# A hi/lo-split attention and gated MLP kernel: a new order for its whole program, from the first loads on, and eleven operations that change engine

## The chip, the cores and the metric

One core of a Trainium2 chip runs the kernel. The metric is the device time in microseconds (us) of one execution. The kernel before takes 412.66 us, the median of three runs (412.56 to 412.87).

## The reference

All arithmetic is float32; S = 2048 tokens, D = 512, F = 1376, 32 heads of 16.

```python
xn = layernorm(x)
q, k, v = split_heads(xn @ wqkv)                # 32 heads, Dh = 16
idx = pos[:, None] - arange(8) * 2              # window 8, dilation 2, causal
logits = einsum("bhsd,bhswd->bhsw", q, k[idx]) * Dh ** -0.5
s = einsum("bhsw,bhswd->bhsd", softmax(logits), v[idx]) @ wo
g = silu(gelu(layernorm(xn) @ w1 + b1) @ w2 + b2)
out = x + s * g
```

## The kernel before

**Split operands.** The large matmuls run in f16. Each operand is kept as a high half, the value rounded to f16, and a low half, what is left. A product is the sum of three matmuls: high by high, low by high, high by low. So each tile of an operand costs a pass for its high half (on ScalarE, or by table on VectorE or GpSimd) and one for its low half (mostly on VectorE).

**Tiles and stages.** The 2048 tokens are taken as two dilation halves of 8 tiles of 128 tokens. The 512 columns of q, k and v are taken as 4 head blocks; head block and half make 8 attention units. Of each unit TensorE makes q, k and v of the 8 tiles (`qkv`, matmul L864: 12 per tile, 384 columns, 480 where one head block also carries a piece of the MLP's last columns), and the PSUM result is evicted with its scale into the array `U`, on VectorE (L878) or ScalarE (L882, and L886 for the extra 96 columns). For units 0 and 1 the tables `EV0` and `EV1` name the engine per tile; from unit 2 on it is ScalarE. Logits, softmax (Exp at L956) and weighted sums run on VectorE and GpSimd. The MLP runs beside this in 4 chunks of 512 tokens: `mlp1` makes a block of h (L1143, 12 matmuls of 512 columns), ScalarE applies Gelu in PSUM (L1156) and writes the high half (L1159), `mlp2` multiplies by w2 (L1186). L1056 and L1088 are the output product with wo. The PSUM tiles of L864, L1143 and L1056 come from one ring of three buffers, ps0 to ps2.

**The opening.** Loads are issued by SyncE in one queue: `t` (L1258, 256 KB) is a tile of x that comes transposed, for tiles 6 and 7; `x` (L1233, 256 KB) is a tile of x in rows; `q` (L588, 384 KB) is a quarter of wqkv for head block 0; `w` (L1260) are pieces of w1. Tiles 6 and 7 take the direct way: their mean is made on VectorE (L685) and one matmul (L691), or for tile 7 with four matmuls (L682); L693 subtracts it, and L700 multiplies float32 x by float32 wqkv, one matmul per tile and quarter (two records each in the trace). The other tiles get statistics on VectorE (L659, L660), a power on GpSimd (L718), a normalisation (L748 on GpSimd, L742 and L744 on ScalarE, or L751 on VectorE), and a transpose on TensorE (L766, four per tile), whose result is split into halves in `yT` (L770 ScalarE or L772 VectorE for the high half, by `HI_ENG`; L773 for the low). The square sums of wqkv's quarters are made on ScalarE (L597) and summed on TensorE (L513); VectorE makes a power of two of them (L524 to L542), by which the high halves of wqkv are scaled (L619). Before the data come, TensorE runs 19 matmuls of no use (L1305). w1's high halves are made by `split` on ScalarE (L565) or VectorE (L563), by the table `W1ENG`.

**What sets the order.** Each operation is entered into a plan with its engine, reads and writes. `Plan.issue` then emits all of them in the sequence that the long table `ORDER` gives, one number per operation. Each engine's program is that sequence, cut down to its own instructions, and the buffers of a ring are handed out in it as well, so ORDER also decides which PSUM buffer a product gets. At run time each engine works through its list in order and waits by semaphores.

```python
HI_ENG = ('act', 'act', 'act', 'dve', 'dve', 'dve', 'dve', 'act')      # L53
W1ENG = ('act', 'dve', 'act', 'act', 'act', 'act', 'act')              # L57
EV0 = ('act', 'dve', 'dve', 'act', 'act', 'act', 'dve', 'dve')         # L62
EV1 = ('dve', 'dve', 'act', 'act', 'act', 'act', 'dve', 'act')         # L63
order, fixed = [], [self.ops[n] for n in reversed(ORDER)]              # Plan.issue
```

## Time and profile before

| | |
|---|---|
| timed runs, median (lowest to highest) | 412.66 us (412.56 to 412.87) |
| profiled execution: span, first to last instruction | 411.0 us |
| TensorE (PE) busy, matmuls | 402.8 us, 98%, 2030 records |
| VectorE (DVE) busy | 381.6 us, 93% |
| ScalarE (ACT) busy | 224.9 us, 55% |
| GpSimd (POOL) busy | 132.7 us, 32% |

The page gives a span for the profiled execution and no time beyond it; the median of the runs is 1.66 us longer than that span. Busy shares are means over the whole span: ScalarE, at 55% overall, is full in some stretches and idle in others. In a timeline row the figure in brackets is how long the engine stood idle before the row, and what ended that. The start times of successive rows on TensorE show its pace better than the durations, since a matmul's record reaches into the next one's.

### The profile page before, as it was taken

Reading aid. Unit: us, or ns where it says so; the run is one execution under the profiler, and the core shown is the slowest. Engines: PE = TensorE matmul, PEld = TensorE weight load, DVE = VectorE, ACT = ScalarE, POOL = GpSimd, SP = SyncE. Lnnn points to the kernel's source line nnn. Section 1 sums busy time; section 2 is a strip of 40 time slices with the busy share of each in tenths; the row PEclk is TensorE's granted clock in tenths of the full one; section 3 lists DMA queues with packets and bytes.
Section 4 is the critical chain, followed back from the end, with each engine's and each line's share of the span. In section 5 each row is a group of like instructions: output and inputs, shape, how many; then the busy total and the mean of one; then the engine's idle time right before and its main releaser. Section 6 shows DMA issues by size and latency. Waiting matters only on the chain.

```text
span 411.0 us, 5490 instructions
## 1 busy us (share of the span) xinstructions
PE 402.8 (98%) x2030; PEld 198.7 (48%) x2030; DVE 381.6 (93%) x386; ACT 224.9 (55%) x372; POOL 132.7 (32%) x141
## 2 busy tenths in 40 slices
PE   7899999999999999999999999999999999999996
PEld 4565544444444455445544554444445544444443
DVE  4899999999999999999889999899999989989985
ACT  3899987983989736633564164214523177236310
POOL 2843000053562425143424243233322505250012
PEclk9999999999999999999999999999999999999999
DMA  8957538251018372911251009610344452004984
GB/s 288 395 104 227 177 90 214 92 179 27 1 30 189 85 130 77 150 49 27 51 141 27 0 2 213 209 50 22 107 122 120 107 135 60 0 1 116 285 214 162
DMA packets 52627, 48.04 MB, mean 117 GB/s; under 512 B 37066, under 2 KB 37510, under 8 KB 52088
## 3 DMA queue, kind: packets, MB, share of 16 engines
...
q8 instruction: 16, 0.26, 0.3%
...
## 4 chain that ended last, share of the span: by engine, by line
PE 90%; DVE 3%; ACT 3%; DMA 1%; POOL 1%; issue 0%; SPq 0%; POOLq 0%; ACTq 0%; DVEq 0%
PE ps L864 27%; PE z L1186 25%; PE ps L1143 25%; PE ps L1056 5%; PE z L1088 2%; PE ps L1088 2%; PE z L1174 2%; DMA prod<-in_A_x_dram 1%; DVE bn L659 1%; ACT w L565 1%; ACT w L504 1%; PE pl L1088 1%; PE z L1177 1%; PE pl L864 1%; POOL prod L748 1%; DVE yT L773 0%
## 5 line engine op out<-in xcount | busy, mean ns | idle before, releaser
L864 PE MATMUL ps<-wq,yT 128*128 128x384 f16 (+1 forms) x708 | 128.9, 337 | 0.2
L1186 PE MATMUL z<-w,h 128*128 128x512 f16 x480 | 111.4, 379 | 0.0
L1143 PE MATMUL ps<-yT,w 128*128 128x512 f16 x480 | 109.0, 379 | 0.0
L864 PEld LDWEIGHTS <-yT 128*128 128x128 f16 x744 | 72.2, 98 | 59.1 <-issue 1.3
L930 DVE TENSOR_TENSOR prod<-U 128x2048 f32<-128x2048 f32 x32 | 73.8, 2312 | 4.1 <-ACT U L882 3.0
L1143 PEld LDWEIGHTS <-w 128*128 128x128 f16 x480 | 46.8, 98 | 55.6 <-issue 0.5
L933 DVE TENSOR_REDUCE L<-prod 128x128 f32<-128x2048 f32 x32 | 73.0, 2282 | 0.5
L1186 PEld LDWEIGHTS <-h 128*128 128x128 f16 x480 | 46.5, 98 | 54.6 <-issue 0.7
L999 POOL TENSOR_TENSOR prod<-prod,prod 128x1024 f32<-128x1024 f32 x14 | 41.3, 2968 | 81.3 <-DVE prod L988 81.3
L882 ACT ACTIVATE U<-ps,cs 128x384 f32<-128x384 f32 x54 | 30.1, 575 | 62.9 <-PE ps L864 62.7
L988 DVE TENSOR_TENSOR prod<-pl,U 128x2048 f32<-128x2048 f32 x28 | 63.5, 2283 | 0.3
L1156 ACT ACTIVATE ps<-ps,b1T,hsc 128x512 f32<-128x512 f32 x40 | 29.8, 747 | 37.0 <-PE ps L1143 36.8
L1159 ACT ACTIVATE h<-ps,hsc 128x512 f16<-128x512 f32 x40 | 27.4, 684 | 20.6 <-PE z L1186 19.7
L1009 POOL COPY gate<-prod 1x1 f32<-1x1 f32 x21 | 4.6, 219 | 102.2 <-DVE prod L930 102.2
L1010 POOL TENSOR_TENSOR prod<-prod 128x1024 f32<-128x1024 f32 x14 | 32.9, 2348 | 0.0
L1161 DVE SCALAR_TENSOR_TENSOR h<-ps,hsc,h 128x512 f16<-128x512 f32 x40 | 29.5, 744 | 3.2 <-ACT h L1159 3.2
L1056 PE MATMUL ps<-wo,oT 128*128 128x512 f16 x96 | 21.5, 379 | 0.0
L983 DVE TENSOR_TENSOR prod<-prod,prod 128x2048 f32<-128x2048 f32 x9 | 20.6, 2288 | 0.2
L971 ACT ACTIVATE o<-prod,osc 128x1024 f16<-128x1024 f32 (+1 forms) x9 | 9.5, 1051 | 18.0 <-DVE prod L983 9.9
L1010 POOL TENSOR_TENSOR prod<-prod,prod 128x1024 f32<-128x1024 f32 x7 | 16.4, 2347 | 0.0
L1088 PEld LDWEIGHTS <-oT 128*128 128x128 f16 x108 | 10.5, 98 | 10.4 <-issue 0.2
L1056 PEld LDWEIGHTS <-oT 128*128 128x128 f16 x96 | 9.4, 98 | 11.1
...
## 6 DMA issues: line engine op xcount, KB each, us to landing
...
```

The source lines that it names most:

```text
L864: nc.tensor.matmul(b.t[:, 0:wide], y[:, s, k, o:o + P], wq[hb][:, t, k], start=(n == 0), stop=(n == 11))
L882: act(384, lambda i=i, b=b: nc.scalar.activation(U3[:, i:i + 31:15, :], b.t[:, 0:384].rearrange("p (t e) -> p t e", t=3), AF.Identity, sca ...
L930: dve(2048, lambda p2=p2, g=g: nc.vector.tensor_tensor(p2(), q, slots(Ut, KH, 2 * g), op=ALU.mult), qk + [("kh", ub, 0), ("kh", ub, 1), (" ...
L933: dve(2048, lambda pr=pr, g=g: nc.vector.tensor_reduce(L3()[:, 2 * g:2 * g + 2], pr.t.rearrange("p (r f d) -> p r f d", r=2, d=DH), AX.X, ...
L988: dve(2048, lambda: nc.vector.tensor_tensor(pr.t.rearrange("p (r f d) -> p r f d", r=2, d=DH), A3()[:, 2 * g:2 * g + 2].rearrange("p r (f ...
L999: pool(2.4, lambda n=n: nc.gpsimd.tensor_tensor(acc.t[:, n:n + 1024], acc.t[:, n:n + 1024], p1.t[:, n:n + 1024], op=ALU.add), [acc, p1], [ ...
L1010: nc.gpsimd.tensor_tensor(x.t[:, 0:1024], x.t[:, 0:1024], y(), op=ALU.add)
L1056: nc.tensor.matmul(b.t, oT[:, hb, i // 4, s, i % 4], wo[:, t, hb], start=(hb == 0 and n == 0), stop=(hb == last and n == 2))
L1088: nc.tensor.matmul(b.t[:, cols], oT[:, hb, i // 4, s, i % 4], wo[:, t, hb, cols], start=(start and hb == 0 and n == 0), stop=(stop and hb ...
L1143: nc.tensor.matmul(b.t[0:M], w1[:, s, f * 512 + k * M:f * 512 + (k + 1) * M], yT[ch][:, t, k], start=(n == 0), stop=(n == 11))
L1156: act(512, lambda: nc.scalar.activation(b.t[0:M], b.t[0:M], AF.Gelu_apprx_tanh, bias=b1T[0:M, f:f + 1], scale=hsc[0:M, 1:2]), [b, ("b1T",) ...
L1186: nc.tensor.matmul(z.t, hl[s][:, t * P:(t + 1) * P], w2[:, w, f], start=(f == 0 and n == 0), stop=False)
```

## The change

The table ORDER is replaced as a whole, so that every engine's program has another sequence of the same operations. Three high halves and eight evictions change engine by table: the high half of tile 3 and the evictions of unit 0's tiles 1 and 2 and unit 1's tiles 1 and 6, among others; the number of evictions that VectorE makes in units 0 and 1 is 7 of 16 before and after. The other new tables (`SUBS`, `ST_ENG`, `YLO`, `SECS`, `QH0`, `QH1`, `LASTC`) hold values by which the code does what it did before. ScalarE's program has 28 table loads where it had 24. Line numbers shift by 6 to 43.

```diff
-HI_ENG = ('act', 'act', 'act', 'dve', 'dve', 'dve', 'dve', 'act')
+HI_ENG = ('act', 'act', 'act', 'act', 'dve', 'dve', 'dve', 'act')
-W1ENG = ('act', 'dve', 'act', 'act', 'act', 'act', 'act')
+W1ENG = ('dve', 'dve', 'act', 'act', 'act', 'dve', 'act')
-EV0 = ('act', 'dve', 'dve', 'act', 'act', 'act', 'dve', 'dve')
-EV1 = ('dve', 'dve', 'act', 'act', 'act', 'act', 'dve', 'act')
+EV0 = ('dve', 'act', 'act', 'act', 'act', 'act', 'dve', 'dve')
+EV1 = ('dve', 'act', 'act', 'dve', 'dve', 'act', 'act', 'dve')
+SUBS = ()
+ST_ENG = ('dve',) * 8
+YLO = ('dve',) * 8
+SECS = BATCHES
+QH0 = ('act', 'act', 'act', 'act')
+QH1 = ('act', 'act')
...
 ORDER = (
-    0, 1, 235, 19, 2, 3, 4, 5, 6, 7, 8, 9, 10, 11, 110, 111, 112, 113, 114, 115, 116, 117, 118, 119, 120, 121,
```

The loads on SyncE's queue at the start of the program (`in_A_xt_dram` is a `t` load, `in_A_wqkv_dram` a `q`, `in_A_x_dram` an `x`; the number on the left of the arrow is the buffer it fills), before:

```order
L1258 DMA U_94<-in_A_xt_dram 128x512
L588 DMA prod_100<-in_A_wqkv_dram 128x768 x2
L1233 DMA prod_101<-in_A_x_dram 128x512 x2
L588 DMA U_94<-in_A_wqkv_dram 128x768
L1258 DMA U_94<-in_A_xt_dram 128x512
```

and after:

```order
L1301 DMA U_94<-in_A_xt_dram 128x512
L1276 DMA prod_100<-in_A_x_dram 128x512
L1301 DMA U_94<-in_A_xt_dram 128x512
L1276 DMA prod_100<-in_A_x_dram 128x512
L594 DMA prod_101<-in_A_wqkv_dram 128x768
L1276 DMA prod_100<-in_A_x_dram 128x512
L594 DMA prod_101<-in_A_wqkv_dram 128x768
L1276 DMA prod_102<-in_A_x_dram 128x512
L594 DMA U_94<-in_A_wqkv_dram 128x768
```

Both `t` loads and two `x` loads now stand ahead of the first quarter of wqkv, which moves from the second place to the fifth, and the third quarter from the sixth to the ninth.

TensorE after its 19 matmuls of no use and the mean of tile 6, before (L700 direct product, L682 mean of tile 7, L766 transposes of a tile, L513 square sums):

```order
L700 MATMUL pl_146<-prod_100,U_94 128x384 x2
...
L700 MATMUL pl_146<-prod_100,U_94 128x384
L682 MATMUL ps_144<-U_94,first 128x128 x4
L700 MATMUL pl_146<-prod_100,U_94 128x384
...
L766 MATMUL z_150<-first,prod_101 128x128 x4
L700 MATMUL z_148<-prod_100,U_94 128x384 x4
L766 MATMUL z_150<-first,prod_101 128x128 x4
```

and after, with the lines L725, L702, L809 and L519 for L700, L682, L766 and L513:

```order
L702 MATMUL ps_144<-U_94,first 128x128 x4
L725 MATMUL pl_146<-prod_101,U_94 128x384
L809 MATMUL z_150<-first,prod_100 128x128 x4
L725 MATMUL z_148<-prod_101,U_94 128x384
L519 LDWEIGHTS fours
L519 MATMUL z_147<-s_125,fours 128x1
L725 MATMUL pl_146<-prod_101,U_94 128x384 x2
L519 LDWEIGHTS fours
L519 MATMUL z_147<-s_125,fours 128x1
L725 MATMUL z_148<-prod_101,U_94 128x384 x2
L809 MATMUL z_150<-first,prod_100 128x128 x4
L725 MATMUL z_148<-prod_101,U_94 128x384
```

The mean of tile 7 goes ahead of all direct products, products of the two direct tiles alternate quarter by quarter, and three transposes of tiles (L809; the third stands two rows further down) come ahead of the first product of `qkv`, where it was two.

ScalarE late in the program (between 280 and 300 us of the span before), after only (L1014, L999, L929, L925, L1199 and L1202 are L971, L956, L886, L882, L1156 and L1159 of before; ps0 to ps2 are the three PSUM buffers of the ring):

```order
L999 ACT_TABLE_LOAD
L999 ACTIVATE L1_111<-L1_111 128x512
L929 ACTIVATE first_65<-ps1_144,hsc_158 128x96
L925 ACTIVATE U0_93<-ps1_144,cs0_118 128x3x128
L1199 ACT_TABLE_LOAD
L1199 ACTIVATE ps0_143<-ps0_143,b1T_97,hsc_158 128x512
L925 ACTIVATE U0_93<-ps2_145,cs0_118 128x3x128
L1202 ACTIVATE h1_114<-ps0_143,hsc_158 128x512
L929 ACTIVATE hl0_98<-ps2_145,hsc_158 128x96
L925 ACTIVATE U0_93<-ps1_144,cs0_118 128x3x128
```

TensorE's program there fills ps2 with a tile of `qkv`, ps1 with another, ps0 with a block of `mlp1`, ps1 again with `qkv`, and then writes the output product (L1099, which is L1056) into ps2. The two evictions of ps2 stand behind the Gelu of ps0.

## Rows read from the trace of the kernel before

**Rows 1.** The page: its first line, and busy time per engine with share of the span.

```profile
span 411.0 us, 5490 instructions
...
PE 402.8 (98%) x2030; PEld 198.7 (48%) x2030; DVE 381.6 (93%) x386; ACT 224.9 (55%) x372; POOL 132.7 (32%) x141
```

**Rows 2.** Windows: stretch, length, busy us per engine (instructions), granted clock, DMA share, GB/s.

```profile
0.00:20.00 20.00, 15.85 (x75) 9.64 (x76) 12.95 (x42) 11.99 (x22) 11.23 (x20) 1.00 0.93 346
20.00:50.00 30.00, 29.87 (x180) 17.25 (x178) 28.31 (x53) 28.91 (x55) 8.29 (x6) 1.00 0.65 177
50.00:400.00 350.00, 349.91 (x1739) 168.06 (x1738) 333.92 (x283) 183.99 (x298) 110.28 (x114) 1.00 0.38 97
```

**Rows 3.** Timeline of TensorE, 0 to 20: start, duration, engine, line, operation, [idle before, releaser].

```profile
1.19 3.57 PE L1305 MATMUL z<-first,fours 128*128 128x256 bf16 x16 [1.19 <-DVE first L440]
...
6.21 1.56 PE L700 MATMUL pl<-prod,U 128*128 128x384 f32 x4 [0.27 <-DVE U L693]
...
8.07 0.16 PE L513 MATMUL z<-s,fours 128*128 128x1 bf16 x1 [0.29 <-ACT wq L597]
...
10.12 1.16 PE L682 MATMUL ps<-U,first 128*128 128x128 f32 x8 [1.14 <-DMA U<-in_A_xt_dram]
11.11 0.81 PE L700 MATMUL pl<-prod,U 128*128 128x384 f32 x2
...
12.61 0.66 PE L766 MATMUL z<-first,prod 128*128 128x128 f32 x4 [0.69 <-POOL prod L748]
13.11 2.75 PE L700 MATMUL z<-prod,U 128*128 128x384 f32 x8
...
16.33 1.46 PE L864 MATMUL ps<-wq,yT 128*128 128x384 f16 x8
18.24 0.66 PE L766 MATMUL z<-first,prod 128*128 128x128 f32 x4 [0.45 <-DVE ssq L524]
```

**Rows 4.** Timeline of ScalarE, 4 to 12.

```profile
4.54 0.84 ACT L597 ACTIVATE wq<-prod 128x768 bf16<-128x768 f32 x1 [2.53 <-DMA prod<-in_A_wqkv_dram]
...
7.08 0.84 ACT L597 ACTIVATE wq<-prod 128x768 bf16<-128x768 f32 x1 [1.60 <-DMA prod<-in_A_wqkv_dram]
...
9.42 0.84 ACT L597 ACTIVATE wq<-U 128x768 bf16<-128x768 f32 x1 [1.41 <-DMA U<-in_A_wqkv_dram]
...
10.26 2.12 ACT L619 ACTIVATE wq<-prod,qsc 128x384 f16<-128x384 f32 x4
```

**Rows 5.** Timeline of VectorE, 3 to 12.

```profile
7.76 0.69 DVE L659 BATCH_NORM_STATS2 bn<-prod 128x6 f32<-128x512 f32 x1 [1.60 <-DMA prod<-in_A_x_dram]
```

**Rows 6.** Timeline of GpSimd, 5 to 16.

```profile
10.49 2.07 POOL L748 TENSOR_SCALAR prod<-prod,mv,rb 128x512 f32<-128x512 f32 x1
```

**Rows 7.** Timeline of ScalarE, 285 to 300.

```profile
290.94 1.28 ACT L1156 ACT_TABLE_LOAD   x1 [1.14 <-PE ps L1143]
292.23 0.75 ACT L1156 ACTIVATE ps<-ps,b1T,hsc 128x512 f32<-128x512 f32 x1
293.32 0.34 ACT L886 ACTIVATE hl<-ps,hsc 128x96 f32<-128x96 f32 x1 [0.34 <-PE ps L864]
293.56 0.57 ACT L882 ACTIVATE U<-ps,cs 128x384 f32<-128x384 f32 x1
294.03 0.69 ACT L1159 ACTIVATE h<-ps,hsc 128x512 f16<-128x512 f32 x1
```

**Rows 8.** Chain of waits, in order of time: start, duration, what.

```profile
62.50 2.59 PE ps L1143 x12
...
267.21 4.86 PE ps L864 x24
```

**Rows 9.** Groups by line and shape: busy us, mean ns of one, idle before.

```profile
L1143 PE MATMUL ps<-yT,w 128*128 128x512 f16 x480 | 109.0, 379 | 0.0
...
L569 DVE SCALAR_TENSOR_TENSOR w<-yT,zsc,w 128x1024 f16<-128x1024 f32 x4 | 5.0, 1275 | 0.0
...
L563 DVE TENSOR_SCALAR w<-oT,hsc 128x512 f16<-128x512 f32 x1 | 0.5, 486 | 0.0
```

More of the change, by code (lines that the diff above doesn't have):

```diff
@@ L32 @@
 NFB = 7
-LASTP = 256
+LASTC = (0, 256, 512)
 LASTPOOL = (0, 2, 4)
@@ L671, in tile_mixer, with parts, xcs @@
     xt = {i: U[1][:, XT[n] * P:(XT[n] + 4) * P].rearrange("p (k t) -> p k t", k=KT) for n, i in enumerate(FP)}
+    def parts(i):
+        return ((0, 1), (1, KT)) if i in SUBS else ((0, KT),)
+    def xcs(i):
+        return [("xc", i, k0) for k0, k1 in parts(i)]
     def center(i):
@@ L691, in center @@
             pe(1, P, lambda: nc.tensor.matmul(b.t[:, 0:P], mean1, f3()[:, 0], start=True, stop=True), [f], [b], fp32=6, prio=PMEAN)
-        m = lambda: b.t[:, 0:P].rearrange("p (o t) -> p o t", o=1).to_broadcast([P, KT, P])
-        dve(512, lambda: nc.vector.tensor_tensor(x3, x3, m(), op=ALU.subtract), [b, ("xt", i)], [("xc", i)], port=False, c=0.16)
+        for k0, k1 in parts(i):
+            m = lambda k0=k0, k1=k1: b.t[:, 0:P].rearrange("p (o t) -> p o t", o=1).to_broadcast([P, k1 - k0, P])
+            dve(P * (k1 - k0), lambda k0=k0, k1=k1, m=m: nc.vector.tensor_tensor(
+                x3[:, k0:k1], x3[:, k0:k1], m(), op=ALU.subtract), [b, ("xt", i)], [("xc", i, k0)], port=False, c=0.16)
     pb = {}
     def direct(i):
-        b = pb[i] = ([R_pl] + R_z[1:])[FP.index(i)].new()
+        b = pb[i] = ([R_pl] + R_z[1:] + R_z[:1] + [R_ps] * 3)[FP.index(i)].new()
         for k in range(KT):
@@ L701, in direct @@
                 b.t[:, 0:384], xt[i][:, k], stq[0]()[:, k * 384:(k + 1) * 384], start=(k == 0), stop=(k == KT - 1)),
-                [("xc" if i in XC else "xt", i), ("stq", 0, k)], [b], fp32=4.5, holds=stkey[0], after=pl.users([b]))
+                [("xc", i, max(k0 for k0, k1 in parts(i) if k0 <= k)), ("stq", 0, k)], [b], fp32=4.5, holds=stkey[0], after=pl.users([b]))
     mv0 = sb.tile([P, NI, 2], F32, name="mv0")
@@ L706, in tile_mixer, with stats_act @@
     gof = {i: g for g in GROUPS for i in g}
+    def stats_act(i):
+        q, (x, xkey) = cpos[i], xk[i]
+        sm = R_s.new()
+        o, dst = (i % 4) * P, yT[i // 4]
+        junk = dst[:, 0, :, o:o + P].bitcast(BF16)
+        act(512, lambda: nc.scalar.activation(x(), x(), AF.Identity, accum_out=sm.t[:, 0:1]), [xkey], [xkey, (sm, 0)], aps=2)
+        act(1, lambda: nc.scalar.activation(mv0[:, q, 0:1], sm.t[:, 0:1], AF.Identity, scale=1.0 / D), [(sm, 0)], [("mv0", i)])
+        act(1, lambda: nc.scalar.activation(sm.t[:, 1:2], sm.t[:, 0:1], AF.Identity, scale=-D ** -1.5), [(sm, 0)], [(sm, 1)])
+        act(512, lambda: nc.scalar.activation(
+            junk, x().rearrange("p (k t) -> p k t", k=KT), AF.Square, bias=sm.t[:, 1:2], scale=D ** -0.5,
+            accum_out=mv0[:, q, 1:2]), [xkey, (sm, 1), ("mv0", i)], [("mv0", i), ("yh", 0, i)], aps=3)
     def ln0(g):
@@ L710, in ln0 @@
         for i in g:
+            if ST_ENG[i] == "act":
+                stats_act(i)
+                continue
             with pl.fuse():
@@ L756, in y0 @@
             act(512, lambda: nc.scalar.copy(v16()[:, 0], x()), [yk, xkey], [(y16, 0)], aps=0)
-            dve(512, lambda: nc.vector.tensor_tensor(v16()[:, 1], x(), v16()[:, 0], op=ALU.subtract), [yk, xkey, (y16, 0)], [y16])
+            if YLO[i] == "dve":
+                dve(512, lambda: nc.vector.tensor_tensor(v16()[:, 1], x(), v16()[:, 0], op=ALU.subtract), [yk, xkey, (y16, 0)], [y16])
+            else:
+                pool(1.161, lambda: nc.gpsimd.tensor_tensor(v16()[:, 1], x(), v16()[:, 0], op=ALU.subtract), [yk, xkey, (y16, 0)], [y16])
             dma(P * 2048, lambda: nc.sync.dma_start_transpose(
@@ L851, in qkv @@
         cp = lambda i: cpos[i] if c == 0 else i
-        raw = pl.users([("xc", j) for j in FP]) if u == 1 else set()
+        raw = pl.users([x for j in FP for x in xcs(j)]) if u == 1 else set()
         wide = 384 + FL * (hb == HLAST)
@@ L1090, in mm @@
             return go
-        parts = [(i, slice(0, D)) for i in range(NI - 1)] + [(NI - 1, slice(0, LASTP)), (NI - 1, slice(LASTP, D))]
+        parts = [(i, slice(0, D)) for i in range(NI - 1)] + [(NI - 1, slice(a, b)) for a, b in zip(LASTC, LASTC[1:])]
         banks = {}
@@ L1291, in tile_mixer @@
                     y0(i)
-    for n, g in enumerate(BATCHES):
+    for n, g in enumerate(SECS):
         with prio(PSEC[n]):
```

25 lines of the change are left out of this document (18 added, 7 removed), and 123 rows, old and new, of the table ORDER.

## The prediction, made before the changed kernel ran

> **What bounds the kernel now.** I read the page first, then the busy time by stretch, then the timelines of the opening, then the late stretch where the new order looks tight.
>
> By the page TensorE's matmuls fill 402.8 of 411.0 us [rows 1]; what else the chip does can cost or give time only through TensorE's idle time. The stretches say where that lies [rows 2]: in the first 20 us TensorE is busy for 15.85, from 20 to 50 for 29.87 of 30, from 50 to 400 for 349.91 of 350. So 4.15 us are idle in the opening (1.19 of them before the first matmul), and 0.22 in the 380 us behind it. The change has the same matmuls. The end is therefore the opening's waits, plus fixed work, plus whatever new waits the other order makes in a program that so far has next to none. The stretch from 20 to 50 is the tightest: ScalarE is busy for 28.91 of 30 there, VectorE for 28.31 [rows 2].
>
> The timeline of the opening names five waits [rows 3]: 0.27 for the centred tile 6, 0.29 for ScalarE's square sums, 1.14 for tile 7's load, 0.69 for GpSimd's normalisation, 0.45 for VectorE: 2.84 together. A record runs on while the next starts, so a wait is really longer than shown: 12 matmuls of 512 columns take 2.59, 0.216 each [rows 8], and the mean record of them lasts 0.379 [rows 9], 0.16 more. The first real product, L864, starts at 16.33 [rows 3], and two sets of transposes (L766) are done by then.
>
> **When the loads come.** The landings show in the engines that wait for them. After 0.63 MB (`t` of tile 6 and the first quarter of wqkv) ScalarE starts at 4.54; after 1.0 MB, at 7.08; after 1.88 MB, at 9.42 [rows 4]. The first `x` is there at 7.76, after 1.25 MB [rows 5], tile 7 at 10.12, after 2.13 MB [rows 3]. So 256 KB take about 0.68, 384 KB about 1.0, and one step, to 1.0 MB, took 2.54, some 1.5 too many. I take the same landing for the same amount of bytes in the new order: two `t` and two `x` are 1.0 MB, at 7.1, and the first quarter, at 1.38 MB, comes a third of a microsecond behind the 7.76, at **8.1**. If that delay does not come ahead of it, it lands at 6.6; if a delay of the same size comes again, 9.6. Both ends go into the range.
>
> **TensorE's opening, step by step.** Up to tile 6's mean nothing changes: TensorE ends it at 5.9 by its record (6.21 less the 0.27 of waiting [rows 3]), some 5.7 by its pace. Then comes tile 7's mean (L682 to L702), whose data lie at 0.75 MB and so land between 4.9 and 6.4; it takes 0.99 (10.12 to 11.11 [rows 3]), until 6.7. TensorE then waits for the first quarter until 8.1: 1.4 us, one wait in the place of four. From there it has eight products of tile and quarter (two records are one of them: 0.81 at 11.11, less the 0.16 that runs on, 0.65 [rows 3]) and three sets of transposes (12.61 to 13.11, 0.50 each [rows 3]): 8.1 + 5.2 + 1.5 = 14.8 for the first L864, against 16.33, with a set of transposes (0.50) more behind it. That is **2.0 ahead**.
>
> Is each thing there? The first transpose stands one product behind, at 8.8. Tile 0's `x`, at 0.5 MB, lands by 4.5; statistics as at 7.76, 0.69 and about 0.5 more [rows 5] and the power on GpSimd let the normalisation start near 6.5; with 2.07 [rows 6] it ends at 8.5. That cover is 0.3 us; with the load 0.3 later TensorE waits there. The second quarter follows at 9.8, the third at 11.4, ahead of the products by the new sequence. The square sums come later than before by about 2 us, for the second quarter's L597 now starts at 9.8 instead of 7.08 [rows 4], and VectorE's power of two came 2.2 after the sum's matmul (8.07 to the first L619 at 10.26 [rows 3, 4]), with a normalisation to fill ScalarE's time: the four scaled high halves, 2.12 [rows 4], run from about 12.3 to 14.4, 0.4 before the first L864.
>
> Behind the first L864 I see one wait left, TensorE's for the next square sums, at 0.45 as shown with its hidden 0.16, like the 0.45 at 18.24 [rows 3]: nothing gained or lost. The 0.22 idle of 20 to 400 is, if it lies in four pieces, each with 0.16 hidden, 0.9; of the new order I take one such piece to be left, 0.2: **0.7 gained**, bounds 0 and 0.9. Opening and middle together: 2.0 + 0.7 = 2.7.
>
> **What switches engine.** Eight evictions change sides, seven of sixteen stay on VectorE: nothing on balance. Three high halves go one from VectorE to ScalarE, two the other way. Of these two, 512 columns take 0.49 on VectorE and the 1024 have no row there: between twice that, 0.97, and 1.28, the price of a 1024-column pass with two operands [rows 9]; I take 1.0, the nearer operation. VectorE has 1.69 us free in 20 to 50 [rows 2]; +1.0 goes into it, but in the wrong place it stops an eviction: from 0 to 1.0, I take 0.
>
> **What the new order loses.** Late in the program TensorE's output product goes into the buffer ps2, whose last readers on ScalarE stand behind the Gelu of another block (the last of the three order lists). When that block's last matmul ends, ScalarE still has the table load, the Gelu, one eviction of 384 columns, the high half and one of 96 columns before ps2 is free: 1.29 (290.94 to 292.23), 0.75, 0.47 (293.56 to 294.03), 0.69 and 0.34 [rows 7], 3.54, less 0.1 for the overlap of high half and eviction, 3.4. TensorE meanwhile has one group of 12 matmuls of 480 columns, 2.43 (half of the 24 in 4.86 [rows 8]). The wait is **1.0**; its bounds are 0.8, if the table load starts early, and 1.4, if an Exp in front runs late. In the old order that eviction had no Gelu ahead of it, and TensorE no wait. A second place of the kind, an output product that waits for VectorE's low half of a block, costs 0 to 0.69, what the same pass takes on ScalarE (L1159 [rows 7]); I take 0.2, since VectorE starts it beside ScalarE. Four table loads are added. Where none of TensorE's buffers hangs on them they cost nothing: ScalarE is busy for 55% [rows 1].
>
> The Trainium skill ("ScalarE: Activation LUTs", What ACT_TABLE_LOAD costs) speaks against this order: it adds a drain of 1.38 us to the load's 1.28, 2.66 per switch. By that the wait above would be 2.4 and the time 412.5. The row says otherwise: from the load's start to the Gelu's is 1.29 [rows 7], with no drain between.
>
> **The sum.** 411.0 of span - 2.7 + 1.2 = 409.5. The timed median lies 1.66 above the profiled span, and the runs within 0.3 of each other, so I carry the 1.66 over: **411.1 us** (412.66 - 1.5 = 411.16).
>
> **The rivals.** (1) *The opening's lead is eaten in 20 to 50.* ScalarE and VectorE are full there [rows 2], and TensorE arriving 2.0 earlier only waits for their evictions instead. For: 1.09 and 1.69 us free in 30. Against: both also start earlier, since the loads of x come first. If two thirds of 2.7 go, 412.66 - 0.9 + 1.2 = 413.0; without the 1.2 of losses, 411.8. About 412.4.
>
> (2) *Slower: the added table loads stand on the path.* Each of the four costs 1.29 [rows 7]; where a PSUM buffer that TensorE wants is evicted behind each, with one group's cover of 2.43 or less, all four are paid: 5.2 - 2.7 = 2.5, 415.2. It decides from three loads on (two, 2.6, cancel the gain). For: three buffers for all products. Against: I found one such place, not four.
>
> (3) *The clock.* The granted clock reads 1.00 in all stretches [rows 2], yet 16 of the matmuls of no use, 256 columns each, take 3.57, 0.22 each [rows 3], which is the 1.2 GHz level, and 512 columns later 0.216 [rows 8], the 2.4 GHz level. The opening up to about 5.7 ran at the lower one. Should TensorE fall back to it in its 1.4 us wait and need as long again, 4.5 us (1.19 to 5.7), it would do half of the work in them: +2.25, 413.4. Against: the products behind the 1.14 wait at 10.12 go at the old pace, 0.81 for two records at 11.11 [rows 3]. The Trainium skill ("TensorE: Matmul & The Clock Gate", What's actually happening) says that an idle array falls to half clock; the trace shows no fall after a wait of that size.
>
> (4) *More gain:* the delayed step does not come ahead of the first quarter, which lands at 6.6, and TensorE waits for nothing until GpSimd's tile at 8.5: 1.0 to 1.3 more, 409.9.
>
> **How the numbers follow.** My forecast as summed, 410.4 to 412.0: 0.52, of which 0.05 above 411.83. Rival 1: 0.22, of which 0.05 below 411.83. Rival 2: 0.11. Rival 3: 0.04, half of it above 413.49. Rival 4: 0.11. What a measurement can tell from no change is 0.2%, 0.83 us: faster is below 411.83, slower above 413.49. Faster: 0.47 + 0.05 + 0.11 = 0.63; slower: 0.11 + 0.02 = 0.13, less 0.02 of rival 2 where only two loads are paid, 0.11; the rest, 0.26, within. The range reaches down to the extra gain, 409.4, and up to 413.3, the edge of rivals 1 and 3; left out are rival 2 and a little below.
>
> **What would show it.** Right: the first L907 (the new L864) near 14.8 with twelve transposes before it, one wait of about 1.4 near 6.7 that a load of wqkv ends, an idle of about 1.0 before an output product near 290 ended by ScalarE, and under 0.3 idle from 20 to 280. Wrong: the first quarter landing at 9 or later, TensorE idle in 20 to 50 behind evictions, a wait behind each new table load, or products L725 at twice the 0.65 behind the wait.

## The result: 0.27% slower, and the profile after

The changed kernel takes **413.51 us** (median of 10 runs, 412.87 to 415.1), the kernel before, run beside it, 412.61 (10 runs, 411.92 to 412.93). The ratio is 1.0027, 95% interval 1.0015 to 1.0038. The forecast was 411.1 and faster; it was wrong in sign, and the time lies above its range. The profiled execution of the changed kernel is the slowest of its ten, 415.1 us with a span of 413.3 and a mean granted clock of 0.994; the other nine have spans of 411.1 to 412.1 at 0.998 to 1.000, so what this profile shows of the clock belongs to it alone among the ten.

The page: TensorE's work is the same, the span longer [rows 1].

```profile
span 413.3 us, 5510 instructions
...
PE 403.5 (98%) x2030; PEld 199.9 (48%) x2030; DVE 380.7 (92%) x387; ACT 227.3 (55%) x375; POOL 131.8 (32%) x141
```

The windows show where TensorE stands idle (columns as in [rows 2]: stretch, length, busy us of PE, PEld, DVE, ACT, POOL, granted clock, DMA share, GB/s). First the kernel before, in the stretches that turned out to matter:

```profile
20.00:45.00 25.00, 24.87 (x152) 14.43 (x150) 23.31 (x51) 23.91 (x42) 8.29 (x6) 1.00 0.70 180
45.00:62.00 17.00, 17.00 (x87) 8.32 (x86) 16.90 (x16) 15.39 (x29) 0.48 (x6) 1.00 0.34 110
```

and the changed kernel:

```profile
0.00:20.00 20.00, 17.15 (x80) 11.36 (x81) 13.22 (x44) 10.50 (x21) 10.80 (x20) 0.91 0.91 333
20.00:45.00 25.00, 25.00 (x153) 14.70 (x152) 21.17 (x47) 23.73 (x43) 9.22 (x6) 1.00 0.69 178
45.00:62.00 17.00, 15.44 (x77) 7.25 (x75) 16.73 (x16) 15.55 (x32) 0.98 (x1) 1.00 0.42 132
62.00:250.00 188.00, 188.00 (x953) 91.78 (x951) 178.15 (x159) 117.07 (x198) 64.35 (x69) 1.00 0.34 82
250.00:400.00 150.00, 148.39 (x725) 70.01 (x724) 142.15 (x110) 60.35 (x87) 41.81 (x44) 1.00 0.40 109
```

The opening's idle time went from 4.15 us to 2.85, as forecast in sign. But 1.56 us are idle between 45 and 62, where there were none, and 1.61 between 250 and 400. Those 3.2 us are three waits. TensorE's timeline names each with what ended it:

```profile
48.72 0.81 PE L907 MATMUL ps<-wq,yT 128*128 128x384 f16 x4 [1.56 <-DVE U L921]
...
264.27 2.75 PE L1099 MATMUL ps<-wo,oT 128*128 128x512 f16 x12 [0.55 <-DVE h L1204]
...
296.10 2.75 PE L1099 MATMUL ps<-wo,oT 128*128 128x512 f16 x12 [1.05 <-ACT hl L929]
```

**The wait at 48.72** is the unforeseen one: a tile of `qkv` waits for a ring buffer, which VectorE frees late. VectorE, just before:

```profile
38.88 3.14 DVE L575 SCALAR_TENSOR_TENSOR w<-oT,hsc,w 128x512 f16<-128x512 f32 x3
41.94 2.06 DVE L575 SCALAR_TENSOR_TENSOR w<-o,hsc,w 128x1024 f16<-128x1024 f32 x1
45.17 2.97 DVE L973 TENSOR_TENSOR prod<-U 128x2048 f32<-128x2048 f32 x1 [1.17 <-DMA U<-U]
48.06 0.60 DVE L921 TENSOR_SCALAR U<-ps,cs 128x384 f32<-128x384 f32 x1
48.59 2.27 DVE L976 TENSOR_REDUCE L<-prod 128x128 f32<-128x2048 f32 x1
```

VectorE waits 1.17 for the halo transfer of `U` (L939: rows of k and v copied between partitions), then does the 2048-column product L973, and only then the eviction L921 that TensorE wants. By the two programs it is the eviction of tile 7 of unit 1, one of the eight that change engine (`EV1`): in the old order ScalarE makes it, and VectorE's last eviction, of another tile, stands ahead of the products. The kernel before:

```profile
50.77 0.57 ACT L882 ACTIVATE U<-ps,cs 128x384 f32<-128x384 f32 x1
```

```profile
42.89 0.62 DVE L878 TENSOR_SCALAR U<-ps,cs 128x384 f32<-128x384 f32 x1 [0.43 <-PE ps L864]
43.42 6.68 DVE L930 TENSOR_TENSOR prod<-U 128x2048 f32<-128x2048 f32 x3
```

GpSimd's two passes, which ran from 33.05 to 36.39 before, come beside VectorE's long ones now:

```profile
40.27 2.65 POOL L559 TENSOR_SCALAR oT<-oT,hsc 128x1024 f32<-128x1024 f32 x1 [14.66 <-ACT w L571]
43.01 2.97 POOL L560 TENSOR_TENSOR w<-oT,w 128x1024 f16<-128x1024 f32 x1
```

Both engines are slowed: the same two passes took 1.12 and 2.13 in the kernel before, the 1024-column L575 took 1.28 [rows 9] and takes 2.06, and L973 takes 2.97 where the next ones take 2.28.

The halo is not what sets the eviction's time. In e2 below, whose program is the same up to here, the product starts without a wait for it, at 41.83, and takes 4.22; GpSimd, VectorE and TensorE there:

```profile
40.93 2.98 POOL L560 TENSOR_TENSOR w<-oT,w 128x1024 f16<-128x1024 f32 x1
```

```profile
41.83 4.22 DVE L973 TENSOR_TENSOR prod<-U 128x2048 f32<-128x2048 f32 x1
45.97 0.60 DVE L921 TENSOR_SCALAR U<-ps,cs 128x384 f32<-128x384 f32 x1
```

```profile
46.63 0.81 PE L907 MATMUL ps<-wq,yT 128*128 128x384 f16 x4 [1.57 <-DVE U L921]
```

The product ends 2.14 behind GpSimd's second pass, as it does in the profile after (2.16), in e3 (2.14) and in e8 (2.15), whenever the halo came. Nor does the wait hang on the lead. It is 1.56 in the profile after, where the clock (below) had cost 1.7 of the lead and the first L907 came at 16.87, and 1.57, 1.56 and 1.57 in e2, e3 and e8, where it came at 14.77, 14.62 and 14.97. By these rows the new order makes it, with the eviction behind the product and GpSimd's passes beside it. No run put tile 7 back to ScalarE.

**The wait at 296.10** is the forecast one, step by step as it was worked out; ScalarE:

```profile
292.69 1.28 ACT L1199 ACT_TABLE_LOAD   x1 [1.22 <-PE ps L1186]
293.99 0.75 ACT L1199 ACTIVATE ps<-ps,b1T,hsc 128x512 f32<-128x512 f32 x1
294.67 0.57 ACT L925 ACTIVATE U<-ps,cs 128x384 f32<-128x384 f32 x1
295.13 0.69 ACT L1202 ACTIVATE h<-ps,hsc 128x512 f16<-128x512 f32 x1
295.70 0.35 ACT L929 ACTIVATE hl<-ps,hsc 128x96 f32<-128x96 f32 x1
```

From 292.69 to 296.05 are 3.36 us (forecast 3.4), and the wait is 1.05 (forecast 1.0).

**The opening**, TensorE to 20 us [rows 3]:

```profile
6.66 1.16 PE L702 MATMUL ps<-U,first 128*128 128x128 f32 x8 [0.98 <-DMA U<-in_A_xt_dram]
8.41 1.24 PE L725 MATMUL pl<-prod,U 128*128 128x384 f32 x2 [0.60 <-DMA prod<-in_A_wqkv_dram]
9.45 1.06 PE L809 MATMUL z<-first,prod 128*128 128x128 f32 x4
10.30 1.49 PE L725 MATMUL z<-prod,U 128*128 128x384 f32 x2
...
13.33 1.54 PE L725 MATMUL z<-prod,U 128*128 128x384 f32 x4
...
16.87 1.46 PE L907 MATMUL ps<-wq,yT 128*128 128x384 f16 x8
```

Two loads end two waits, 0.98 and 0.60, in the place of the one of 1.4. Then products and transposes go at half pace for some 3 us (a pair of L725 in 1.49 where it takes 0.81), and the first L907 comes at 16.87, not at 14.8. The windows of one us show why; the third number from the end is the granted clock:

```profile
7.00:8.00 1.00, 0.81 (x8) 0.62 (x6) 0.66 (x1) 0.00 (x0) 1.00 (x1) 1.00 1.03 368
8.00:9.00 1.00, 0.59 (x2) 0.49 (x3) 0.85 (x4) 0.70 (x1) 0.41 (x1) 0.90 1.01 400
9.00:10.00 1.00, 1.00 (x5) 0.59 (x4) 0.93 (x4) 0.23 (x2) 0.00 (x0) 0.50 1.03 406
...
12.00:13.00 1.00, 1.00 (x4) 0.54 (x4) 0.64 (x2) 0.96 (x2) 0.00 (x0) 0.89 1.06 409
```

TensorE had stood idle twice; the clock then fell to 0.50, the 1.2 GHz level, and was back near 12. That cost this one execution 1.7 us: from the L725 at 8.41 to the one at 13.33 are 4.92 us, and the same stretch takes 3.24 (8.13 to 11.37) in the profile of e4 below, which keeps the clock. Where the experiments share this opening and the clock stays up, the first L907 stands between 14.6 and 15.2.

### The profile page after: what moved, and what is told of

It reads as the page before. It is cut to its first block, busy times and chain, and to the rows that moved or that the text cites. A ratio compares the mean times of both kernels' runs of the same rounds, so it can differ in the third digit from the quotient of the medians.

```text
span 413.3 us, 5510 instructions
## 1 busy us (share of the span) xinstructions
PE 403.5 (98%) x2030; PEld 199.9 (48%) x2030; DVE 380.7 (92%) x387; ACT 227.3 (55%) x375; POOL 131.8 (32%) x141
## 4 chain that ended last, share of the span: by engine, by line
PE 78%; DVE 10%; ACT 4%; issue 4%; DMA 3%; SPq 1%; DVEq 0%; ACTq 0%
PE ps L907 23%; PE z L1229 21%; PE ps L1186 20%; PE ps L1099 4%; DVE prod L973 2%; PE z L1131 2%; DVE L L976 2%; DVE prod L1031 2%; PE ps L1131 2%; PE z L1217 2%; DMA U<-U 1%; DMA prod<-in_A_wqkv_dram 1%; DVE h L1204 1%; PE pl L907 1%; PE pl L725 1%
## 5 line engine op out<-in xcount | busy, mean ns | idle before, releaser
L907 PE MATMUL ps<-wq,yT 128*128 128x384 f16 (+1 forms) x708 | 129.1, 337 | 1.6 <-DVE U L921 1.6
L1229 PE MATMUL z<-w,h 128*128 128x512 f16 x480 | 113.6, 379 | 0.0
L907 PEld LDWEIGHTS <-yT 128*128 128x128 f16 x744 | 72.4, 98 | 59.9 <-issue 2.1
L973 DVE TENSOR_TENSOR prod<-U 128x2048 f32<-128x2048 f32 x32 | 73.9, 2309 | 5.8 <-ACT ps L1199 3.1
L976 DVE TENSOR_REDUCE L<-prod 128x128 f32<-128x2048 f32 x32 | 72.9, 2282 | 0.5
L925 ACT ACTIVATE U<-ps,cs 128x384 f32<-128x384 f32 x55 | 30.8, 575 | 68.5 <-PE ps L907 66.8
L1042 POOL TENSOR_TENSOR prod<-prod,prod 128x1024 f32<-128x1024 f32 x14 | 38.5, 2768 | 65.8 <-DVE prod L1031 65.8
L1199 ACT ACTIVATE ps<-ps,b1T,hsc 128x512 f32<-128x512 f32 x40 | 29.6, 746 | 27.7 <-PE ps L1186 27.6
L1202 ACT ACTIVATE h<-ps,hsc 128x512 f16<-128x512 f32 x40 | 27.2, 683 | 10.8 <-PE z L1229 9.2
L1204 DVE SCALAR_TENSOR_TENSOR h<-ps,hsc,h 128x512 f16<-128x512 f32 x40 | 29.6, 744 | 3.7 <-ACT h L1202 3.6
L1099 PE MATMUL ps<-wo,oT 128*128 128x512 f16 x96 | 21.9, 379 | 1.6 <-ACT hl L929 1.1
L1014 ACT ACTIVATE o<-prod,osc 128x1024 f16<-128x1024 f32 (+1 forms) x9 | 9.4, 1048 | 19.5 <-DVE prod L1026 11.9
L1053 POOL TENSOR_TENSOR prod<-prod,prod 128x1024 f32<-128x1024 f32 x7 | 16.4, 2348 | 0.0
L1099 PEld LDWEIGHTS <-oT 128*128 128x128 f16 x96 | 9.4, 98 | 13.1 <-issue 2.2
```

Source lines behind the costliest of these rows:

```text
L907: nc.tensor.matmul(b.t[:, 0:wide], y[:, s, k, o:o + P], wq[hb][:, t, k], start=(n == 0), stop=(n == 11))
L925: act(384, lambda i=i, b=b: nc.scalar.activation(U3[:, i:i + 31:15, :], b.t[:, 0:384].rearrange("p (t e) -> p t e", t=3), AF.Identity, sca ...
L973: dve(2048, lambda p2=p2, g=g: nc.vector.tensor_tensor(p2(), q, slots(Ut, KH, 2 * g), op=ALU.mult), qk + [("kh", ub, 0), ("kh", ub, 1), (" ...
L976: dve(2048, lambda pr=pr, g=g: nc.vector.tensor_reduce(L3()[:, 2 * g:2 * g + 2], pr.t.rearrange("p (r f d) -> p r f d", r=2, d=DH), AX.X, ...
L1042: pool(2.4, lambda n=n: nc.gpsimd.tensor_tensor(acc.t[:, n:n + 1024], acc.t[:, n:n + 1024], p1.t[:, n:n + 1024], op=ALU.add), [acc, p1], [ ...
L1053: nc.gpsimd.tensor_tensor(x.t[:, 0:1024], x.t[:, 0:1024], y(), op=ALU.add)
```

## The experiments

Where an expectation names a theory by its letter, "theory A" takes a new wait for a slip of the order that costs what it shows; "theory B" says that VectorE has no time left there, so that a wait moved away comes back elsewhere; "theory C" is the clock; "theory F" says that ScalarE and VectorE are full from 20 to 45 and the opening's lead cannot live there. In the diffs a row is an instruction in its engine's program, and - and + show its move against the changed kernel unless another is named. Every ratio is to the kernel before, with its 95% interval; the changed kernel's is 1.0027.

**e1: the eviction ahead of the product** (VectorE, near 45).

```diff
-L973 TENSOR_TENSOR prod_100<-U_93 128x2048
 L921 TENSOR_SCALAR U_94<-ps_143,cs_119 128x3x128
+L973 TENSOR_TENSOR prod_100<-U_93 128x2048
 L976 TENSOR_REDUCE L_110<-prod_100 128x2x64
```

> The changed kernel with one instruction moved: on VectorE the eviction of the tile of unit 1 that TensorE waited 1.56 us for at 47 us now stands ahead of the 128x2048 product of the logits that itself waits for a transfer until 45.2. Theory A (three new waits behind the opening ate the gain: 1.7 at 47, 0.7 at 263, 1.2 at 295): the wait at 47 falls to under 0.2 and the time from 413.5 to about 411.9, down 1.6. Theory B (VectorE, 92% busy, sets the end; TensorE's wait only moves to a later place, since the logits start about 1 us later): 413.2 to 413.8, with a new wait of over 1 us behind 47. Theory C (the loss is the opening's lower clock): unchanged, 413.5.

Measured: 1.0031 (1.002 to 1.0041), no gain. The wait at 48.72 is gone, and TensorE's timeline has two others instead:

```profile
49.58 0.81 PE L1186 MATMUL ps<-yT,w 128*128 128x512 f16 x3 [1.42 <-DVE h L1204]
...
50.70 0.17 PE L524 MATMUL z<-s,fours 128*128 128x6 bf16 x1 [0.31 <-ACT w L1411]
```

1.73 in the place of 1.56: the low half L1204, which stands behind L973 and L976 on VectorE, is late by what the eviction gained. Not a slip of the order alone, then, but a lack of VectorE's time, so far; 1.98 of that time goes by idle, until TensorE has made the tile that L921 evicts at 43.73.

**e2: ps2 freed ahead of the Gelu** (ScalarE, near 292).

```diff
-L1199 ACT_TABLE_LOAD
-L1199 ACTIVATE ps_143<-ps_143,b1T,hsc 128x512
 L925 ACTIVATE U_93<-ps_145,cs_118 128x3x128
+L929 ACTIVATE hl_98<-ps_145,hsc 128x96
+L1199 ACT_TABLE_LOAD
+L1199 ACTIVATE ps_143<-ps_143,b1T,hsc 128x512
 L1202 ACTIVATE h_114<-ps_143,hsc 128x512
-L929 ACTIVATE hl_98<-ps_145,hsc 128x96
```

> The changed kernel with ScalarE's two evictions of the buffer ps2 moved ahead of the table load and Gelu at 293 us. Theory A: TensorE's wait of 1.05 (1.2 with what its record hides) before the output product at 296 goes, and the time falls from 413.5 to about 412.4. Theory B or C: within 0.3 of 413.5.

Measured: 0.9997 (0.9988 to 1.0005), that is 0.003, 1.2 us, below the changed kernel. The wait is gone and nothing takes its place: this one was a slip of the order.

**e3: the low half ahead of the weighted sum** (VectorE, near 262).

```diff
+L1204 SCALAR_TENSOR_TENSOR h_113<-ps_144,hsc,h_113 128x512
 L1031 TENSOR_TENSOR prod_101<-pl_146,U_93 128x2048
-L1204 SCALAR_TENSOR_TENSOR h_113<-ps_144,hsc,h_113 128x512
```

> The changed kernel with VectorE's low half of the block in ps1 moved ahead of a 2.3 us product at 261 us. Theory A: TensorE's wait of 0.55 (0.7 with what is hidden) before the output product at 264 goes; 413.5 to about 412.9. Theory B: the product behind it starts 0.7 later and VectorE gives it back, 413.3 to 413.8. Theory C: 413.5.

Measured: 1.0016 (1.0008 to 1.0025), 0.0011, 0.45 us, below the changed kernel. The wait of 0.55 is gone; VectorE's order cost it, not its load. (Its profile also shows a wait of 0.76 at 51.27 for the square sums of w2, of which e5 tells more.)

**e4: the three moves of e1, e2 and e3 together.**

> All three moves at once. Theory A: they add, 1.6 + 1.1 + 0.6 = 3.3, so about 410.2, some 2.4 below the kernel before at 412.6, which is then what the opening and the small waits of the middle gave. Theory B: above 412.5. Theory C: 413.5.

Measured: 1.0 (0.9986 to 1.0015), 411.84 us, of 12 runs two at 413.95 and 414.48, with mean granted clocks of 0.994 and 0.995 where the other ten have 0.998 or more. With the late waits gone the kernel is as fast as before, and no faster: the opening's lead is still missing. TensorE shows e1's wait of 1.42 and one more of 0.39 for L1204 at 55.62.

**e5: e4, and the two low halves ahead of the long passes** (VectorE, 47 to 55; against e4).

```diff
-L976 TENSOR_REDUCE L_110<-prod_100 128x2x64
 L1204 SCALAR_TENSOR_TENSOR h_114<-ps_145,hsc,h_114 128x512
+L976 TENSOR_REDUCE L_110<-prod_100 128x2x64
...
+L1204 SCALAR_TENSOR_TENSOR h_115<-ps_144,hsc,h_115 128x512
 L973 TENSOR_TENSOR prod_102<-U_93 128x2048
-L1204 SCALAR_TENSOR_TENSOR h_115<-ps_144,hsc,h_115 128x512
```

> The kernel with all three moves, and two more on VectorE: the low halves (L1204) that free the buffers of the first blocks of the MLP go ahead of the 128x2048 reduction and product that stood before them, at 47 and 52 us. Theory D (a matter of order on VectorE alone: short passes that TensorE waits for stand behind long ones): TensorE's wait of 1.42 at 49.9 and of 0.39 at 55.6 go, and the ratio to the kernel before falls from 1.000 to about 0.9955, 1.9 us less. Theory B (VectorE has no time left there; what is moved back is late next): a new wait of 1 us or more on VectorE between 55 and 65, and a ratio of 0.998 to 1.000.

Measured: 0.9999 (0.9986 to 1.0012). VectorE's waits shrink to 0.46, and another engine's takes their place:

```profile
50.78 0.17 PE L524 MATMUL z<-s,fours 128*128 128x6 bf16 x1 [1.66 <-ACT w L1411]
```

These are the square sums of w2 on ScalarE. They stand behind L510, which waits for the last big load of w2; ScalarE in the same run:

```profile
46.88 1.91 ACT L510 ACTIVATE w<-yT 128x2048 bf16<-128x2048 f32 x1 [1.67 <-DMA yT<-in_B_w_dram]
```

From here a second limit was suspected behind VectorE: that load.

**e6: GpSimd's passes earlier** (ScalarE's high half that GpSimd waits for goes ahead, near 34).

```diff
+L571 ACTIVATE w_86<-oT,hsc 128x1024 x2
+L925 ACTIVATE U_93<-pl_146,cs_118 128x3x128
 L571 ACTIVATE w_86<-oT,hsc 128x1024
-L925 ACTIVATE U_93<-pl_146,cs_118 128x3x128
-L571 ACTIVATE w_86<-oT,hsc 128x1024 x2
```

> The changed kernel with one of ScalarE's high halves of w1 (the one that GpSimd's low half waits for) moved from the last to the first place of four, as it stood in the kernel before. GpSimd's two passes then start near 35.5 in place of 38.0 (or 40.3 in the profile of the changed kernel). Theory E (GpSimd's passes beside VectorE's long ones make both slow: 2.06 for 1.28, 2.97 to 4.22 for 2.30, and that makes the eviction late): the product ahead of the eviction goes back to 2.3, TensorE's wait of 1.56 falls to 0.4 to 0.8, and the time by 0.8 to 1.2, ratio to before from 1.0027 to about 1.000. Rival (the transfer of the halo sets that product's start and the eviction's time): ratio unchanged within 0.001 and the product at its start of now.

Measured: 1.0063 (1.0048 to 1.0077), slower. GpSimd's passes ran at 36.06 in 1.12 and 2.18, and L973 fell to 2.28; but VectorE's three L575, now beside them, took 4.89 for 3.14, and the eviction on ScalarE that the halo transfer waits for was moved back with the rest. TensorE waited 0.89 and 1.89 between 45 and 53, the second time for ScalarE's square sums of w2. The slowing is real and goes where the passes go. This move brought no gain; since it moved that eviction too, it does not say what earlier passes alone are worth.

**e7: the new opening alone.** The first 130 of the 1264 numbers of the new ORDER, all others as in the kernel before, with its tables but for tile 3's high half and the evictions of unit 0's tiles 0 and 1 (the diff is against the kernel before).

```diff
-HI_ENG = ('act', 'act', 'act', 'dve', 'dve', 'dve', 'dve', 'act')
+HI_ENG = ('act', 'act', 'act', 'act', 'dve', 'dve', 'dve', 'act')
-EV0 = ('act', 'dve', 'dve', 'act', 'act', 'act', 'dve', 'dve')
+EV0 = ('dve', 'act', 'dve', 'act', 'act', 'act', 'dve', 'dve')
```

> The opening alone: the first 130 of 1264 operations in the changed sequence (the loads, tiles 6 and 7, the first transposes, up to about 20 us) and all others in the sequence of before, each group with its own engines. Theory F (the opening's lead of 2 us is lost between 20 and 50 because ScalarE and VectorE are full there, whatever the order): the first product of qkv starts near 14.5 to 15.2 against 16.33, new waits of together 1.5 us or more between 24 and 45, and a ratio of 0.998 to 1.001. Theory A in its wider form (the lead is lost only through places that the new order made): few new waits, ratio near 0.995.

Measured: 0.9992 (0.9984 to 1.0001), no difference that can be told. The first L907 stands at 14.84, 1.5 us ahead of before with a set of transposes more done, and the lead is gone by 35, in these two waits and one of 0.17 at 34.63, with 0.16 hidden in each 2.0 us:

```profile
23.89 3.41 PE L907 MATMUL ps<-wq,yT 128*128 128x384 f16 x20 [0.90 <-ACT U L925]
...
30.40 2.11 PE L907 MATMUL pl<-wq,yT 128*128 128x384 f16 x12 [0.48 <-ACT U L925]
```

So in the old order the lead is lost too, in another place and to another engine.

**e8: TensorE kept awake.** Eight and six more matmuls of no use (L1348) ahead of the two waits of the opening.

```diff
-        pl.add("pe", 0.2, lambda b=b: nc.tensor.matmul(b.t[:, 0:2 * P], fours, mean1.bitcast(BF16), start=True,
-                                                       stop=True), [], [b], prio=1e9)
+        pl.add("pe", 0.2, lambda b=b, n=n: [nc.tensor.matmul(b.t[:, 0:2 * P], fours, mean1.bitcast(BF16), start=True,
+                 stop=True) for m in range({17: 9, 18: 6}.get(n, 1))], [], [b], prio=1e9)
```

> The changed kernel with the waits of the opening filled: 8 more of the matmuls of no use before the mean of tile 7 and 6 of them between it and the first direct product, some 0.107 us each. Theory C (in part of the runs the clock falls to its lower level after these waits, which cost 1.7 us in the profile of the changed kernel): no run above the others by 1.5 us or more, granted clock 1.00 from 5.7 on, median 0.1 to 0.4 lower, ratio to before 1.0018 to 1.0025. Rival (the fall is independent of these waits): one or two runs of twelve above 415 again, ratio 1.0027.

Measured: 1.0048 (1.0036 to 1.006) in five runs, 413.59 to 414.83. None lies far out, and the profile keeps the clock at 1.00, but the median is above the changed kernel's. One row of its profile bears on that, a wait late in the program, 0.52 as shown, for a transposing transfer of the attention's output; the profile after has none there:

```profile
402.63 4.39 PE L1131 MATMUL z<-wo,oT 128*128 128x512 f16 x21 [0.52 <-DMA oT<-o]
```

Whether the added matmuls brought it about, and whether the other four runs have it, is open. As a test of what the clock costs on the average it failed; from the profile after, a fall costs 1.7 us, and one of the ten runs shows it.

**e9: e5, and the last big load of w2 ahead of the halo transfer** (SyncE's queue, against e5), and **e10: that move alone** in the changed kernel.

```diff
+L1307 DMA yT_92<-in_B_w_dram 128x2048
 L939 DMA U_93<-U_93 15x896
 L939 DMA U_93<-U_93 112x896
 L1313 DMA f_104<-in_B_w_dram 128x512
-L1307 DMA yT_92<-in_B_w_dram 128x2048
```

> The kernel of e5_low_half_early with one load more moved: on SyncE's queue the second 1 MB piece of w2 (L1307) goes ahead of the two halo transfers, which wait until 36.2 for unit 0's last eviction and keep what stands behind them waiting, though the transfer engines are idle for a third of 35 to 40. Theory G (behind VectorE's order the next limit is w2's landing: ScalarE stood idle for 1.67 before its squares at 46.9, three small squares queued behind, and TensorE for 1.66 at 50.8): both waits go to under 0.4, the span from 410.3 to about 408.8, ratio to before from 1.000 to about 0.996. Theory B (VectorE has no time left between 45 and 62 whatever comes early; the halo lands later too): TensorE's wait moves to a low half of VectorE between 50 and 62, ratio 0.998 to 1.001.

> The changed kernel with that one load moved and nothing else. Theory G with VectorE's order still in front: the wait of 1.56 behind the eviction at 45 to 47 stays (or grows by what the halo lands later, up to 1), the one before the squares of w2 (0.76 in e3, 0.31 in e1) goes; ratio 1.0015 to 1.0027 against 1.0027 of the changed kernel. Rival (w2's landing alone held TensorE, the eviction's wait is absorbed behind it): ratio 0.999 or lower.

Measured, e9: 1.0006 (0.9995 to 1.0018). The wait for the square sums falls to 0.19, and three of VectorE's come: 0.30 at 48.62, 0.43 at 57.76, 0.88 at 61.82, with the halo 1.10 late at 45.61. Take away one limit and the other holds the same time. e10: 1.0086 (1.0047 to 1.0125), 413.49 to 419.59 us, above what either theory expected. In its profile the halo came 5.39 late, and TensorE stood:

```profile
50.45 1.44 PE L907 MATMUL ps<-wq,yT 128*128 128x384 f16 x4 [5.10 <-DVE U L921]
```

The four matmuls behind that wait took 1.44 where they take 0.81; the granted clock from 50 to 54 is 0.50.

**e11: e4 with half of unit 0's logits left out on VectorE**, and **e12: the same in the kernel before.** For unit 0 L973 and L976 take 1024 columns in place of 2048, and the logits that are missing are copied from the others.

```diff
+        nr = 1 if u == 0 else 2
+        def red(pr, g):
+            nc.vector.tensor_reduce(
+                L3()[:, 2 * g:2 * g + nr], pr.t[:, 0:1024 * nr].rearrange("p (r f d) -> p r f d", r=nr, d=DH),
+                AX.X, ALU.add)
+            if u == 0:
+                nc.vector.tensor_copy(L3()[:, 2 * g + 1], L3()[:, 2 * g])
```

> The kernel of e4_all_three (the changed kernel with the three moves), in which attention unit 0 has half of its work on VectorE left out: each of its four products L973 and sums L976 takes 1024 columns in place of 2048, and the missing logits are copied from the others. Unit 0's logits are wrong by that. VectorE gets some 1.0 us back for each of these eight passes, four of which (4 us) stand between 44 and 57 us in e4. Theory B (the lead of the opening is lost because VectorE has no time left from 44 us on): e4's waits of 1.42 for the low half at 49.6 and 0.39 at 55.6, some 2.1 us with what the records hide, go; 411.84 - 2.1 = 409.7, ratio to the kernel before 0.994 to 0.996. Rival (something else stands behind VectorE at once, ScalarE's square sums L1411 or the loads of w2): a wait that ScalarE or a load ends takes their place, ratio 0.998 to 1.0.

> The kernel before with the same half of unit 0's work left out on VectorE. Theory B: TensorE waits for nothing between 20 and 62 us in the kernel before, so VectorE's spare 4 us there buy nothing: ratio 0.999 to 1.0, and e11 below it by the opening's 2.1 to 2.4 us. Rival (VectorE's load costs time in both orders, and the lead has no part in it): as far below the kernel before as e11, ratio 0.994 to 0.997.

Measured, e11: 0.9976 (0.9957 to 0.9994), 411.21, spread from 409.46 to 413.77. e12: 0.9997 (0.9988 to 1.0007). Less work on VectorE is worth nothing in the old order and some 0.2% in the new one. In e11's profile no wait for VectorE is left, and the second limit stands in its place; TensorE, then ScalarE:

```profile
51.11 0.17 PE L524 MATMUL z<-s,fours 128*128 128x6 bf16 x1 [1.85 <-ACT w L1421]
```

```profile
47.22 1.91 ACT L510 ACTIVATE w<-yT 128x2048 bf16<-128x2048 f32 x1 [1.86 <-DMA yT<-in_B_w_dram]
```

The load was issued at 39.12 and landed at 47.22. So the theory's 409.7 was met in the best run alone; the rival's mechanism showed in the profile.

**e13: both limits out of the way**, e9 with e11's half left out, and **e14: e7 with two evictions on ScalarE ahead of the work that delayed them** (against e7).

```diff
+L925 ACTIVATE U_93<-ps_144,cs_118 128x3x128
 L510 ACTIVATE w_86,s_130<-oT 128x2048
-L925 ACTIVATE U_93<-ps_144,cs_118 128x3x128
...
+L886 ACTIVATE cs_119<-cT,qsc 128x8
 L796 CAST f_107<-prod_102 128x512
-L886 ACTIVATE cs_119<-cT,qsc 128x8
+L925 ACTIVATE U_94<-pl_146,cs_119 128x3x128
 L510 ACTIVATE junk,s_131<-b1T 128x11
-L925 ACTIVATE U_94<-pl_146,cs_119 128x3x128
```

> e9_w2_before_halo with the same half of unit 0's work left out on VectorE as in e11. In e11 VectorE's waits were gone, but TensorE waited 1.85 for the square sums of w2, whose last load landed at 47.22; in e9 that load came earlier, and four waits for VectorE and the sums were left. Theory (two limits stand right behind the lead, VectorE's time and the landing of w2; each alone eats most of it): with both out of the way no wait above 0.3 is left between 45 and 62, TensorE ends 2 us ahead of e4, 409.5 to 410.2, ratio 0.993 to 0.996. Rival (the lead is lost for a third reason, whatever is taken away): a wait of 1.5 or more ended by another engine or load, ratio 0.998 to 1.0.

> e7_opening_alone with two evictions on ScalarE moved ahead of work that nobody waits for at once: the one that TensorE waited for at 23.89 goes ahead of a square sum of w1 (1.9 us), the one at 30.40 ahead of a transposition copy and a small square sum. Theory F (ScalarE is full between 20 and 45, so what is not waited for in one place is waited for in the next): the waits of 0.90 and 0.48 go, but the square sums of w1 end no earlier, and TensorE waits for them, or for the next eviction, instead: ratio 0.998 to 1.0. Rival (only ScalarE's order costs the lead there): 1.4 us and what the records hide go, ratio 0.994 to 0.996.

Measured, e13: **0.9954** (0.9939 to 0.997), 410.53 us, the ratio as expected and the time 0.3 above; all six runs lie below the kernel before's lowest, 411.8. The stretch from 45 to 62, and the one wait left in it:

```profile
45.00:62.00 17.00, 16.14 (x79) 7.54 (x78) 13.57 (x19) 16.09 (x30) 0.00 (x0) 1.00 0.28 81
```

```profile
49.74 0.17 PE L524 MATMUL z<-s,fours 128*128 128x6 bf16 x1 [0.86 <-ACT w L1421]
```

The lead lives when both are gone; the wait of 0.86, more than the 0.3 expected, is for w2's small loads behind the big one. e14: 1.0002 (0.9994 to 1.0011), nothing gained. The wait of 0.90 became one of 0.71, ended by VectorE (which had waited for ScalarE's casts), and the 0.48 became 0.34 and 0.43:

```profile
26.95 2.11 PE L907 MATMUL pl<-wq,yT 128*128 128x384 f16 x12 [0.71 <-DVE U L921]
...
30.34 2.11 PE L907 MATMUL pl<-wq,yT 128*128 128x384 f16 x12 [0.34 <-ACT U L925]
...
34.95 2.11 PE L907 MATMUL pl<-wq,yT 128*128 128x384 f16 x12 [0.43 <-ACT U L925]
```

No version that computes the whole reference beats the kernel before by more than its interval; e2, e4, e5 and e7 are level with it.

## Why the prediction was wrong

**The opening: right.** The prediction had the first L907 at 14.8 with one more set of transposes done, 2.0 ahead. With the clock kept it stands at 14.91 in e4 and 14.70 in e13: 1.42 and 1.63 ahead of 16.33, and 0.50 of transposes more. The terms inside were less exact: tile 7's load came at 6.66 in the profile after, outside the 4.9 to 6.4 (6.08 in e4), and the wait of 1.4 was two, of 0.98 and 0.60 (0.32 and 0.90 in e4; a single one of 1.31 in e11 and 1.55 in e7).

**The loss at 290: right.** Forecast 1.0, shown 1.05, taken away by e2 for 1.2 us.

**The second place: undersized.** Taken at 0.2 of bounds 0 to 0.69 because "VectorE starts it beside ScalarE"; shown 0.55, and e3 is 0.45 us lower. On VectorE a pass of 2.29 stood ahead of the low half, and the nearest row was the wrong one to take.

**The middle and the evictions that switch engine: these steps failed.** "Of the new order I take one such piece to be left, 0.2: 0.7 gained, bounds 0 and 0.9." TensorE lost 1.56 there as shown, about 1.7 with what a record hides, outside the bounds on the side that they didn't have. The bounds were drawn from the idle time of the old order, and that cannot say what TensorE waits for in the new one. The eight evictions that change sides were put at "nothing on balance", since VectorE keeps seven of sixteen; the count says nothing of their places, and tile 7's, new on VectorE, is the one that TensorE waits 1.56 for.

Behind this wait, the lead meets a full engine. The row that could show it was at hand: VectorE's 1.69 us free in 30 [rows 2] is a mean over 20 to 50, and split at 45 its windows (above) leave 0.10 of 17 us free from 45 to 62. A TensorE that comes 2 us earlier wants its evictions 2 us earlier from an engine that has no gap to give. In the new order VectorE is idle for 3.83 of 25 us from 20 to 45, 1.69 in the old, and cannot use that time: it waits 1.87 for TensorE's own sums and 1.17 for the halo. Of its busy time, 0.78 in L575 and 0.69 in L973 (1.94 in e2) go by behind GpSimd. And e11 shows the big load of w2 as a second limit at the same place.

**Rival 1 came nearest to the mechanism.** That the lead waits for evictions, e11 to e13 bear out from 45 on, with a load as a second limit; that the new order makes a wait of its own there, it did not have. It had 0.22, was priced with most of the losses left out, at 412.4, and was sought in the mean of 20 to 50; its other figure, with two thirds of the lead gone and the losses kept, was 413.0. An estimate from the rows for a run with the clock kept: 2.0 from the opening, some 0.5 from the old order's small waits between 20 and 250 (0.22 shown [rows 2], in two or more pieces with 0.16 hidden in each), against 1.7 at 48.72, 0.7 at 264 and 1.2 at 296: 1.1 slower on balance, 0.9 by the medians. e13 shows that the lead itself was real, e12 that the omitted work is not what pays in it. The earlier load of w2 was not tried in the old order, whose TensorE is busy for 17.00 of 17 us from 45 to 62 as it is.

**Rival 2, the added table loads: did not occur.** One of the 28 loads stood on the path, the one at 292.69, and the old order has that one too (290.94 [rows 7]). It took 1.30 to the Gelu's start, with no drain between. The Trainium skill ("ScalarE: Activation LUTs", What ACT_TABLE_LOAD costs) gives 2.66 us for a switch, drain included; this row does not bear it out.

**Rival 3, the clock: seen, and rare.** "Against: the products behind the 1.14 wait at 10.12 go at the old pace" was one execution's evidence. In the profile after the clock fell after waits of 0.98 and 0.60, in e11 it did not after one of 1.31. Its price was put at 2.25; it was 1.7.
